# Attention on one core: Q of two quads in one load, in rows of 3 KB

## The chip, the cores and the metric

The kernel runs on one core of a Trainium2 chip. Such a core has five engines with a queue each: TensorE (PE in the profile, its weight loads PEld), VectorE (DVE), ScalarE (ACT), GpSimd (POOL) and SyncE (SP), which only issues transfers here, and 16 DMA engines, which move data between the large memory (HBM) and the on-chip memory (SBUF, 128 partitions). The metric is the device time of one execution in microseconds; the median of several runs counts.

## What is computed

Softmax attention over 16 x 32 = 512 heads, each with 192 queries, 1024 keys and a width of 128, in bf16:

```python
B, H, Sq, Sk, D = 16, 32, 192, 1024, 128

def reference(q, k, v):
    scale = q.shape[-1] ** -0.5
    scores = jnp.einsum("bhqd,bhkd->bhqk", q, k) * scale
    p = _softmax(scores, axis=-1)
    return jnp.einsum("bhqk,bhkd->bhqd", p, v)
```

## The kernel before

**Units.** Four heads make a quad; there are 128 quads (NQ), numbered x. A quad's scores (four heads, 1024 keys by 192 queries, keys along the partitions) are made in three pieces, b = 0, 1, 2, so the unit of the pipeline is f = 3x + b, and there are 384 units (NF). The softmax takes no maximum: ScalarE exponentiates the scores, and a column of ones beside V makes the row sums. A check of the sums at the end would start a slower general path, `_general_path`; it isn't entered with these inputs.

**Loads.** SP issues all loads of the steady state from one queue, in a fixed order: for each n, V of quad n+3 (`load_v`, L555), K of quad n+5 (`load_k`, L546), Q of quad n+5 (`load_q`, L531). K and V are 1 MB a quad, Q is 192 KB. Each load fills all 128 partitions: K with 8 KB in one run per partition, V with four runs of 2 KB, Q with one run of 1536 bytes, which is six rows of Q. K, V and Q have five buffers each (NKN, NVS). K waits for a free buffer on s_kx, V on s_pv. Outputs are stored from ScalarE's queue, two quads at a time, in runs of 768 bytes.

**Preparing K and Q.** [...] VectorE turns 32 x 32 blocks of 4-byte words: `turn_k` (L747) turns a third of a quad's K from f_kn to f_kx, and GpSimd's `order` (L607) copies that third from f_kx to its place in f_kt. Q takes one step: `turn_q` (L756) turns a whole quad's Q and writes it straight to its place in f_qt, which has two buffers (R = 2). So Q's turn writes with a scattered pattern. GpSimd also spreads V into rows with the column of ones (`spread`, L616).

**Order on VectorE.** Its loop runs over f. In each turn it normalises unit f-5 (`onorm`: L768 the reciprocal, L772 the product, both read f_o), and then prepares K for unit g = f+3 (AHEAD = 3). `turn_q(x)` comes right ahead of `turn_k(3x+2)`, so half a dozen microseconds after the first third of the same quad's K.

**Order on GpSimd.** For each x: `order(3x)`, the two halves of `spread(x-1)`, `order(3x+1)`, `order(3x+2)`. It runs strictly in that order: if V of quad x-1 isn't there, the next thirds of K wait too.

**Order on TensorE.** For each f: `qk(f)`, the scores (L654), then `pv(f-4)`, the product with V (L683). `qk` first takes what it needs from counters, each by a wait that also subtracts: s_qt (Q turned, for b = 0 only), s_kt (K in place), s_e1 (the score bank is free). `take` is at L637. `pv` takes s_on, which VectorE's normalisation raises: f_o has one buffer, so `pv(f-4)` can't begin before `onorm(f-5)` has read it.

**ScalarE** exponentiates each unit's scores in two instructions (L838, one head, and L841, three heads).

Of the kernel before, what the change touches and what calls it, by code (L numbers as in the profile page):

```python
# [407 lines left out]
U32 = mybir.dt.uint32  # L408
# [12 lines left out]
def _attention_kernel(nc, q, k, v, out):  # L421
# [4 lines left out]
    NQ = NH // 4  # L426
    T = SK // 128
    scale = float(D) ** -0.5
    R = PE_LOOP
    assert NH % 8 == 0 and NQ >= 12  # L430
    NF = 3 * NQ
    LAG = 4
# [3 lines left out]

    AHEAD = 3
    NKN, NVS, NKT, NVP = 5, 5, 2, 2
    GQ = 2
    NSO = 3  # L440
    VB = 136
# [9 lines left out]
    with ExitStack() as outer:  # L451
# [7 lines left out]
        s_out = sem("f_out")  # L459
        s_blank = sem("f_blank")  # L460
        s_kn = [sem("f_kn%d" % i) for i in range(NKN)]
        s_qn = [sem("f_qn%d" % i) for i in range(NKN)]
        s_v = [sem("f_v%d" % i) for i in range(NVS)]
        s_st = [sem("f_st%d" % i) for i in range(NSO)]
        s_kx = sem("f_kx")
        s_qt = sem("f_qt")
        s_kt = sem("f_kt")
        s_vp = sem("f_vp")
        s_qk = sem("f_qk")
# [10 lines left out]
        with ExitStack() as es:  # L480
# [9 lines left out]
            kx = sb("f_kx", [128, 2, 2048], U32)  # L490

            kt = sb("f_kt", [128, NKT, 2 * T, 128, 2], BF16)
            qn = sb("f_qn", [128, NKN, 384], U32)

            qt = sb("f_qt", [128, R, 2, SQ, 2], BF16)
            vs = sb("f_vs", [128, NVS, 4, T * D], BF16)
# [32 lines left out]

            def load_q(e, x):  # L530
                e.dma_start(  # L531
                    qn[:, x % NKN, :],
                    qf[4 * x:4 * x + 4].rearrange("a (j u) d -> (a j) (u d)", u=6).bitcast(U32),
                ).then_inc(s_qn[x % NKN], 16)

            hints = {}

# [3 lines left out]
            @block.sync  # L541
            def _(e):
                def load_k(x, lo=0, hi=32):
                    if x >= NKN:
                        e.wait_ge(s_kx, 3 * (x - NKN) + 3)
                    e.dma_start(  # L546
                        kn[:, x % NKN, 64 * lo:64 * hi],
                        kf[4 * x:4 * x + 4].rearrange("a (j r) d -> (a j) r d", r=32)[:, lo:hi, :]
                        .rearrange("p r d -> p (r d)").bitcast(U32),
                    ).then_inc(s_kn[x % NKN], 16)  # L550

                def load_v(x, lo=0, hi=4):
                    if x >= NVS:
                        e.wait_ge(s_pv, 3 * (x - NVS) + 2 + BLANK)
                    e.dma_start(  # L555
                        vs[:, x % NVS, lo:hi, :],
                        vf[4 * x + lo:4 * x + hi].rearrange("a (m t) d -> m a (t d)", t=T),
                    ).then_inc(s_v[x % NVS], 16)


                load_k(0)
                e.wait_ge(s_blank, 1)
                load_k(1)
                load_q(e, 1)
                load_v(0, 0, 2)
                e.wait_ge(s_qk, PRE + 1)
                load_v(0, 2, 4)
                load_k(2, 0, 16)
                e.wait_ge(s_pv, BLANK - 2)
                load_k(2, 16, 32)  # L570
                load_q(e, 2)
                for n in range(3, NKN):
                    load_v(n - 2)
                    load_k(n)
                    load_q(e, n)
                for n in range(NQ):
                    if n == NQ // 2:
                        hint(e)
                    if n + NKN - 2 < NQ:
                        load_v(n + NKN - 2)  # L580
                    if n + NKN < NQ:
                        load_k(n + NKN)
                        load_q(e, n + NKN)
                for i in range(len(store_at), len(stores)):
                    store(e, i)
            def stored(e):
# [3 lines left out]
            @block.gpsimd  # L590
            def _(gp):
                gp.memset(ones[:], 1.0).then_inc(s_one, 1)  # L592

                def set_v(part):
                    return gp.memset(part.bitcast(U32), 0x3F803F80)  # L595

                set_v(vp[:, 0, 0:2 * T].rearrange("p a d -> p (a d)")).then_inc(s_set, 1)
                set_v(vp[:, 0, 2 * T:].rearrange("p a d -> p (a d)")).then_inc(s_blank, 1)
                set_v(vp[:, 1].rearrange("p a d -> p (a d)"))

                def order(g):
                    x, b = divmod(g, 3)
                    lo, hi = PIECES[b]
                    gp.wait_ge(s_kx, g + 1)
                    if x >= NKT - 1 and b == 0:
                        gp.wait_ge(s_qk, 3 * (x - NKT) + 3 + PRE)
                    gp.tensor_copy(  # L607
                        kt[:, x % NKT].bitcast(U32).rearrange("p U (j s u) c -> p U j s (u c)", s=2, u=2)[:, lo:hi],
                        kx[:, x % 2].rearrange("p (U s j u) -> p U j s u", s=2, j=32, u=2)[:, lo:hi],
                    ).then_inc(s_kt, 1)  # L610

                def spread(x, i):
                    if i == 0:
                        gp.wait_ge(s_v[x % NVS], 16 * (x // NVS + (2 if x % NVS == 0 else 1)))
                        gp.wait_ge(s_pv, 3 * (x - NVP) + 3 + BLANK)
                    gp.tensor_copy(  # L616
                        vp[:, x % NVP, 2 * T * i: 2 * T * i + 2 * T, 0:D].bitcast(U32),
                        vs[:, x % NVS, 2 * i: 2 * i + 2, :].rearrange("p a (t d) -> p (a t) d", d=D).bitcast(U32),
                    ).then_inc(s_vp, 1)

                for x in range(NQ + 1):
                    if x == NQ // 2:
                        hint(gp)
                    if x < NQ:
                        order(3 * x)
                    if x >= 1:
                        for i in range(2):
                            spread(x - 1, i)
                    if x < NQ:
                        order(3 * x + 1)  # L630
                        order(3 * x + 2)

            @block.tensor
            def _(pe):
# [3 lines left out]

                def qk(f):
                    x, b = divmod(f, 3)  # L640
                    if b == 0:
                        take(s_qt, 1)
                    take(s_kt, 1)
                    take(s_e1, 1)
                    ins = None
                    for group in CUTS[b]:
                        for w in range(4):
                            h, c = divmod(w, 2)
                            for g, (t, n0, n1) in enumerate(group):
                                c0 = t * SQ + n0 - 512 * b  # L650
                                for a in range(4):
                                    S = s3_ps[f % 2][:, a - 1, :] if a else s1_ps[:]
                                    r = slice(32 * a, 32 * a + 32)
                                    ins = pe.matmul(  # L654
                                        S[:, c0: c0 + n1 - n0],
                                        kt[r, x % NKT, 2 * t + h, :, c],
                                        qt[r, x % R, h, n0:n1, c],
                                        start=w == 0 and g == 0, stop=w == 3, skip_group_check=True,
                                        tile_position=(32 * a, 0))
                    ins.then_inc(s_qk, 1)  # L660
# [57 lines left out]
            def _(dve):  # L718
# [5 lines left out]
                    ins = clear(low[:, z, :, 1, :])  # L724
                ins.then_inc(s_set, 1)
                clear(qt[:, 1].rearrange("p h q c -> p (h q c)"))
                dve.sem_inc(s_e1, 1 + PRE)
                clear(kt[:, 1, 10:16].rearrange("p U k c -> p (U k c)")).then_inc(s_kt, 1)
                for z in range(2):
                    ins = clear(low[:, z, :, 2, :])  # L730
                ins.then_inc(s_out, 1)
                dve.wait_ge(s_out, 2)
                dve.wait_ge(s_blank, 1)
                dve.sem_inc(s_on, LAG + 1 + PRE)
                where = {}
                for i, (x0, c) in enumerate(stores):
                    for a in range(c):
# [2 lines left out]
                def turn_k(g):  # L740
# [8 lines left out]
                        kn[:, x % NKN].rearrange("p (s u U i) -> p s u U i", s=2, u=2, i=32)[:, :, :, lo:hi],  # L749
                    ).then_inc(s_kx, 1)  # L750

                def turn_q(x):
                    dve.wait_ge(s_qn[x % NKN], 16 * (x // NKN + 1))
                    if x >= R - 1:
                        dve.wait_ge(s_qk, 3 * (x - R) + 3 + PRE)
                    dve.transpose(  # L756
                        qt[:, x % R].bitcast(U32).rearrange("p b (y j u) c -> p u y b (j c)", y=3, u=2),
                        qn[:, x % NKN].rearrange("p (u y b i) -> p u y b i", u=2, y=3, b=2),
                    ).then_inc(s_qt, 1)

                def onorm(s):
                    x, w = divmod(s, 3)
# [35 lines left out]
                for f in range(NF + LAG + 1):  # L798
                    s = f - LAG - 1
                    if f == NF // 2:  # L800
                        hint(dve)
                    if s >= 0:
                        onorm(s)
                        if 0 <= s - EARLY < 3:
                            check(0, 2 * EARLY, 0, s - EARLY)
                    g = f + AHEAD
                    if 5 <= g < NF:
                        x, b = divmod(g, 3)
                        if b == 2 and x >= 2:
                            turn_q(x)  # L810
                        turn_k(g)
                for part in range(3):
                    check(2 * EARLY, 2 * NF, 1, part)
# [70 lines left out]
```

## Time and profile before

| | |
|---|---|
| median of 3 runs | 819.04 us (818.56 to 820.16) |
| the profiled execution: its time | 816.7 us |
| the profiled execution: its span | 815.0 us |
| granted TensorE clock | 0.996 |
| read from HBM, written | 293.60 MB, 25.17 MB |

The span runs from the first to the last instruction; the time of the same execution is 1.7 us longer, and the median of the unprofiled runs lies 4.04 us above the span.

The groups of instructions that the change touches, or that stand beside them (line, engine, operation, what it writes and reads, count; then busy time, mean of one in ns, and the idle time just before them with what ended it):

```profile
L747 DVE STREAM_TRANSPOSE f_kx<-f_kn 128x768 uint32<-128x768 uint32 x256 | 248.6, 972 | 38.4 <-DMA f_kn<-in_k_dram 36.5 <-PE f_s L654 1.1
L607 POOL COPY f_kt<-f_kx 128x768 uint32<-128x768 uint32 x256 | 220.9, 863 | 92.1 <-DVE f_kx L747 90.3 <-PE f_o L683 0.2
L747 DVE STREAM_TRANSPOSE f_kx<-f_kn 128x512 uint32<-128x512 uint32 x128 | 85.8, 670 | 0.0
L607 POOL COPY f_kt<-f_kx 128x512 uint32<-128x512 uint32 x128 | 82.2, 642 | 20.4 <-DVE f_kx L747 20.0
L756 DVE STREAM_TRANSPOSE f_qt<-f_qn 128x384 uint32<-128x384 uint32 x128 | 72.9, 570 | 0.0
```

The transfers (KB each, median us from issue to landing):

```profile
f_kn<-in_k_dram SPq DMA_DIRECT2D x127, 1024.0 KB, 18.1
f_vs<-in_v_dram SPq DMA_DIRECT2D x127, 1024.0 KB, 16.3
f_qn<-in_q_dram SPq DMA_DIRECT2D x127, 192.0 KB, 14.2
out_dram<-f_ob ACTq DMA_DIRECT2D x62, 384.0 KB, 9.5
```

### The profile page before, as it was taken

Reading aid. Unit: us, or ns where it says so; the run is one execution under the profiler, and the core shown is the slowest. Engines: PE = TensorE matmul, PEld = TensorE weight load, DVE = VectorE, ACT = ScalarE, POOL = GpSimd, SP = SyncE. Lnnn points to the kernel's source line nnn. Section 1 sums busy time; section 2 is a strip of 40 time slices with the busy share of each in tenths; the row PEclk is TensorE's granted clock in tenths of the full one; section 3 lists DMA queues with packets and bytes.
Section 4 is the critical chain, followed back from the end, with each engine's and each line's share of the span. In section 5 each row is a group of like instructions: output and inputs, shape, how many; then the busy total and the mean of one; then the engine's idle time right before and its main releaser. Section 6 shows DMA issues by size and latency. Waiting matters only on the chain. (4 is left out here: it accounts for less than half of the span.)

```text
span 815.0 us, 71454 instructions
## 1 busy us (share of the span) xinstructions
PE 802.2 (98%) x32996; PEld 716.0 (88%) x32996; DVE 602.0 (74%) x1293; ACT 749.9 (92%) x772; POOL 553.8 (68%) x648
## 2 busy tenths in 40 slices
PE   8899999999999999999999999999999999999997
PEld 7788888888888888888888888888888888888886
DVE  4677777777777777777777777777777777777775
ACT  6799999999999999999999999999999999999995
POOL 5677677667667766766676676676766766766674
PEclk9999999999999999999999999999999999999999
DMA  7999999999999999999999999999999999999992
GB/s 270 396 401 406 408 404 405 409 403 406 409 403 406 408 403 407 407 405 407 407 403 408 407 404 408 406 406 405 407 406 401 396 409 393 388 406 399 393 379 73
DMA packets 138455, 319.16 MB, mean 392 GB/s; under 512 B 7217, under 2 KB 56369, under 8 KB 122161
## 3 DMA queue, kind: packets, MB, share of 16 engines
q1 hardware_dynamic: 105536, 294.22, 91.9%
q10 hardware_dynamic: 32880, 24.58, 9.0%
q14 instruction: 33, 0.26, 0.1%
q8 instruction: 6, 0.10, 0.1%
HBM read 293.60 MB, written 25.17 MB: 391 GB/s over the span
## 5 line engine op out<-in xcount | busy, mean ns | idle before, releaser
L841 ACT ACTIVATE f_pt<-f_s 128x1536 bf16<-128x1536 f32 x384 | 554.6, 1444 | 0.1
L654 PE MATMUL f_s<-f_qt,f_kt 32*128 32x192 bf16 (+1 forms) x20528 | 423.2, 226 | 7.4 <-PEq L637 7.4
L683 PE MATMUL f_o<-f_vp,f_pt 128*64 128x129 bf16 x12368 | 426.8, 222 | 0.4 <-issue 0.2
L683 PEld LDWEIGHTS f_o<-f_vp,f_pt 128*64 128x64 bf16 x12368 | 363.7, 110 | 49.4 <-issue 22.5
L654 PEld LDWEIGHTS f_s<-f_qt,f_kt 32*128 32x128 bf16 x20528 | 349.4, 92 | 44.0 <-issue 9.1
L607 POOL COPY f_kt<-f_kx 128x768 uint32<-128x768 uint32 (+1 forms) x384 | 298.0, 789 | 112.6 <-DVE f_kx L747 110.3
L747 DVE STREAM_TRANSPOSE f_kx<-f_kn 128x768 uint32<-128x768 uint32 (+1 forms) x384 | 334.3, 871 | 38.4 <-DMA f_kn<-in_k_dram 36.5
L616 POOL COPY f_vp<-f_vs 128x1024 uint32<-128x1024 uint32 x256 | 260.1, 1046 | 137.8 <-DMA f_vs<-in_v_dram 129.7
L838 ACT ACTIVATE f_pt<-f_s 128x512 bf16<-128x512 f32 x384 | 229.3, 597 | 56.4 <-PE f_s L654 13.8
L768 DVE RECIPROCAL f_rinv<-f_o 128x2 f32<-128x2 f32 x381 | 64.2, 168 | 156.1 <-PE f_o L683 154.8
L772 DVE TENSOR_TENSOR f_ob<-f_o,f_rinv 128x256 bf16<-128x256 f32 x381 | 161.6, 424 | 13.3 <-DVE f_rinv L768 0.3
L756 DVE STREAM_TRANSPOSE f_qt<-f_qn 128x384 uint32<-128x384 uint32 x128 | 72.9, 570 | 0.0
L825 ACT ACTIVATE f_pt<-f_ones 128x1536 f32<-128x1536 bf16 x3 | 4.2, 1472 | 0.0
L595 POOL MEMSET f_vp<- 128x1088 uint32 (+1 forms) x3 | 3.8, 1312 | 0.0
L683 PE MATMUL f_s<-f_vp,f_pt 128*64 128x129 bf16 x96 | 3.2, 220 | 0.2 <-issue 0.2
L683 PEld LDWEIGHTS f_s<-f_vp,f_pt 128*64 128x64 bf16 x96 | 2.9, 110 | 0.5 <-issue 0.4
L825 ACT ACT_TABLE_LOAD x1 | 1.3, 1283 | 1.2 <-PEq L869 1.2
L696 PE MATMUL f_o<-f_ones 128*128 128x512 bf16 x2 | 1.0, 622 | 1.1 <-POOL f_ones L592 1.1
L720 DVE MEMSET f_pt<- 128x256 uint32 x4 | 1.1, 272 | 0.9 <-PEq L869 0.9
L768 DVE RECIPROCAL f_rinv<-f_s 128x2 f32<-128x2 f32 x3 | 0.5, 171 | 1.4 <-PE f_s L683 1.4
L713 PE MATMUL f_o<-f_bad,f_ones 128*1 128x1 bf16 x1 | 0.2, 165 | 1.3 <-DVEq L814 1.3
L713 PEld LDWEIGHTS f_o<-f_bad,f_ones 128*1 128x1 bf16 x1 | 0.1, 80 | 1.4 <-DVEq L814 1.4
(15 smaller groups left out, 6.8 us busy)
## 6 DMA issues: line engine op xcount, KB each, us to landing
f_kn<-in_k_dram SPq DMA_DIRECT2D x127, 1024.0 KB, 18.1
f_vs<-in_v_dram SPq DMA_DIRECT2D x127, 1024.0 KB, 16.3
f_qn<-in_q_dram SPq DMA_DIRECT2D x127, 192.0 KB, 14.2
out_dram<-f_ob ACTq DMA_DIRECT2D x62, 384.0 KB, 9.5
f_vs<-in_v_dram SPq DMA_DIRECT2D x2, 512.0 KB, 6.4
f_kn<-in_k_dram SPq DMA_DIRECT2D x2, 512.0 KB, 4.7
out_dram<-f_ob SPq DMA_DIRECT2D x1, 384.0 KB, 3.8
out_dram<-f_ob SPq DMA_DIRECT2D x2, 192.0 KB, 2.1
```

The source lines that it names most:

```text
L595: return gp.memset(part.bitcast(U32), 0x3F803F80)
L607: gp.tensor_copy(kt[:, x % NKT].bitcast(U32).rearrange("p U (j s u) c -> p U j s (u c)", s=2, u=2)[:, lo:hi], kx[:, x % 2].rearrange("p (U ...
L616: gp.tensor_copy(vp[:, x % NVP, 2 * T * i: 2 * T * i + 2 * T, 0:D].bitcast(U32), vs[:, x % NVS, 2 * i: 2 * i + 2, :].rearrange("p a (t d) ...
L654: ins = pe.matmul(S[:, c0: c0 + n1 - n0], kt[r, x % NKT, 2 * t + h, :, c], qt[r, x % R, h, n0:n1, c], start=w == 0 and g == 0, stop=w == 3 ...
L683: ins = pe.matmul(O[64 * z: 64 * z + 64, u, 0:129], pt[:, x % R, 2 * y + z, t * SQ + 64 * j: t * SQ + 64 * j + 64], vp[:, x % NVP, (2 * y ...
L747: dve.transpose(kx[:, x % 2].rearrange("p (U s j u) -> p s u U j", s=2, j=32, u=2)[:, :, :, lo:hi], kn[:, x % NKN].rearrange("p (s u U i) ...
L756: dve.transpose(qt[:, x % R].bitcast(U32).rearrange("p b (y j u) c -> p u y b (j c)", y=3, u=2), qn[:, x % NKN].rearrange("p (u y b i) -> ...
L768: dve.reciprocal(ri, O[:, :, 128]).then_inc(s_rc, 1)
L772: dve.tensor_tensor(ob[:, so, 6 * a + 2 * w: 6 * a + 2 * w + 2, :], O[:, :, 0:128], ri.unsqueeze(2).to_broadcast([128, 2, D]), ALU.mult,). ...
L825: return act.activation(part.bitcast(F32), ones[:, 0:1].to_broadcast([128, 2 * T * SQ // 2]), ACT_FN.Copy)
L838: act.activation(pt[:, x % R, 0, c], s1_ps[:], ACT_FN.Exp, scale=scale).then_inc(s_e1, 1)
L841: act.activation(pt[:, x % R, 1:4, c], s3_ps[f % 2][:], ACT_FN.Exp, scale=scale).then_inc(s_e3, 1)
```

## The change

Quads 0 and 1 keep their own loads of 192 KB and their own turns. From quad 2 on, Q of two quads is loaded at once:

- `load_q2(x)`, for even x, is issued right after K of quad x. It consists of four transfers, one for each 32 partitions. Partition 32a + 2j + h gets 12 rows (3072 bytes in one run) of head a of quad x + h. There are three buffers (NQN) of this double size in place of five of the single size.
- `turn_q2(x)` on VectorE turns these 768 words a partition from f_qn to a new tile f_qx, which has two buffers, without rearranging anything. It is placed ahead of `turn_k(3x-1)`.
- `copy_q(x)` on GpSimd, for every quad from 2 on, copies the 384 words of that quad from f_qx to their places in f_qt. It is placed ahead of `order(3x)`.
- `qk` on TensorE no longer takes s_qt: GpSimd's `order(3x)`, which raises s_kt, comes after `copy_q(x)` on the same engine. For quads 0 and 1 other counters of the start stand in (s_e1 and s_on), whose sums stay the same.

```diff
+    NQN = 3
...
-            qn = sb("f_qn", [128, NKN, 384], U32)
+            qn = sb("f_qn", [128, NQN, 768], U32)
+            qx = sb("f_qx", [128, 2, 768], U32)
...
+            def load_q2(e, x):
+                y = x // 2
+                for a in range(4):
+                    e.dma_start(
+                        qn[32 * a:32 * a + 32, y % NQN, :],
+                        qf[4 * x:4 * x + 8].rearrange("(h a) (j u) d -> a j h (u d)", h=2, u=12)[a].bitcast(U32),
+                    ).then_inc(s_qn[y % NQN], 16)
...
                     if n + NKN < NQ:
                         load_k(n + NKN)
-                        load_q(e, n + NKN)
+                        if (n + NKN) % 2 == 0:
+                            load_q2(e, n + NKN)
...
+                def copy_q(x):
+                    gp.wait_ge(s_qx, x // 2)
+                    gp.wait_ge(s_qk, 3 * (x - R) + 3 + PRE)
+                    gp.tensor_copy(
+                        qt[:, x % R].bitcast(U32).rearrange("p b (y j v) c -> p b y j (v c)", y=3, v=4),
+                        qx[:, x // 2 % 2].rearrange("p (v y b j h) -> p h b y j v", v=4, y=3, b=2, h=2)[:, x % 2])
...
                     if x < NQ:
+                        if x >= 2:
+                            copy_q(x)
                         order(3 * x)
...
-                    if b == 0:
-                        take(s_qt, 1)
                     take(s_kt, 1)
...
+                def turn_q2(x):
+                    y = x // 2
+                    dve.wait_ge(s_qn[y % NQN], 64 * (y // NQN + (1 if y % NQN else 0)))
+                    if y >= 3:
+                        dve.wait_ge(s_qk, 3 * (x - 3) + 1 + PRE)
+                    dve.transpose(
+                        qx[:, y % 2], qn[:, y % NQN],
+                    ).then_inc(s_qx, 1)
...
-                        if b == 2 and x >= 2:
-                            turn_q(x)
+                        if b == 2 and x % 2 == 1 and x + 1 < NQ:
+                            turn_q2(x + 1)
                         turn_k(g)
```

More of the change, by code (lines that the diff above doesn't have):

```diff
@@ L461, in _attention_kernel @@
         s_kn = [sem("f_kn%d" % i) for i in range(NKN)]
-        s_qn = [sem("f_qn%d" % i) for i in range(NKN)]
+        s_q0 = [sem("f_q0%d" % i) for i in range(2)]
+        s_qn = [sem("f_qn%d" % i) for i in range(NQN)]
         s_v = [sem("f_v%d" % i) for i in range(NVS)]
@@ L465, in _attention_kernel @@
         s_kx = sem("f_kx")
-        s_qt = sem("f_qt")
+        s_qx = sem("f_qx")
         s_kt = sem("f_kt")
@@ L531, in load_q @@
                 e.dma_start(
-                    qn[:, x % NKN, :],
+                    qn[:, 0, 384 * x:384 * x + 384],
                     qf[4 * x:4 * x + 4].rearrange("a (j u) d -> (a j) (u d)", u=6).bitcast(U32),
-                ).then_inc(s_qn[x % NKN], 16)
+                ).then_inc(s_q0[x], 16)
+            def load_q2(e, x):
[5 more added lines that the diff above has]
+                    ).then_inc(s_qn[y % NQN], 16)
             hints = {}
@@ L570, in _ @@
                 load_k(2, 16, 32)
-                load_q(e, 2)
+                load_q2(e, 2)
                 for n in range(3, NKN):
@@ L574, in _ @@
                     load_k(n)
-                    load_q(e, n)
+                    if n % 2 == 0:
+                        load_q2(e, n)
                 for n in range(NQ):
@@ L726, in _ @@
                 clear(qt[:, 1].rearrange("p h q c -> p (h q c)"))
-                dve.sem_inc(s_e1, 1 + PRE)
+                dve.sem_inc(s_e1, PRE)
                 clear(kt[:, 1, 10:16].rearrange("p U k c -> p (U k c)")).then_inc(s_kt, 1)
@@ L733, in _ @@
                 dve.wait_ge(s_blank, 1)
-                dve.sem_inc(s_on, LAG + 1 + PRE)
+                dve.sem_inc(s_on, LAG - 1)
                 where = {}
@@ L752, in turn_q @@
                 def turn_q(x):
-                    dve.wait_ge(s_qn[x % NKN], 16 * (x // NKN + 1))
-                    if x >= R - 1:
-                        dve.wait_ge(s_qk, 3 * (x - R) + 3 + PRE)
+                    dve.wait_ge(s_q0[x], 16)
+                    if x == 1:
+                        dve.wait_ge(s_qk, PRE)
                     dve.transpose(
-                        qt[:, x % R].bitcast(U32).rearrange("p b (y j u) c -> p u y b (j c)", y=3, u=2),
-                        qn[:, x % NKN].rearrange("p (u y b i) -> p u y b i", u=2, y=3, b=2),
-                    ).then_inc(s_qt, 1)
+                        qt[:, x].bitcast(U32).rearrange("p b (y j u) c -> p u y b (j c)", y=3, u=2),
+                        qn[:, 0, 384 * x:384 * x + 384].rearrange("p (u y b i) -> p u y b i", u=2, y=3, b=2),
+                    ).then_inc(*((s_on, 2 + PRE) if x else (s_e1, 1)))
+                def turn_q2(x):
[6 more added lines that the diff above has]
+                    ).then_inc(s_qx, 1)
                 def onorm(s):
```

## The prediction

> **What bounds the kernel now.** I read the busy shares and the slices first, then the waits in windows along the run, then the timeline where TensorE stalls, and the DMA rows last.
>
> ```profile
> span 815.0 us, 71454 instructions
> PE 802.2 (98%) x32996; PEld 716.0 (88%) x32996; DVE 602.0 (74%) x1293; ACT 749.9 (92%) x772; POOL 553.8 (68%) x648
> ...
> DMA  7999999999999999999999999999999999999992
> ...
> DMA packets 138455, 319.16 MB, mean 392 GB/s; under 512 B 7217, under 2 KB 56369, under 8 KB 122161
> ...
> q1 hardware_dynamic: 105536, 294.22, 91.9%
> q10 hardware_dynamic: 32880, 24.58, 9.0%
> ```
>
> TensorE and the DMA engines are both full, and a busy TensorE proves little. So I ask who waits, early (100 to 200 us) and late (700 to 815 us):
>
> ```profile
> POOL f_vp L616 <- DMA f_vs<-in_v_dram: 1.3, 4, 0.5
> ```
>
> ```profile
> POOL f_vp L616 <- DMA f_vs<-in_v_dram: 27.0, 16, 2.9
> DVE f_rinv L768 <- PE f_o L683: 16.8, 38, 1.3
> DVE f_kx L747 <- DMA f_kn<-in_k_dram: 9.0, 16, 1.5
> ...
> ACT f_pt L838 <- PE f_s L654: 2.5, 6, 0.8
> ```
>
> Early, loads are no concern and TensorE sets the pace: in the timeline around 400 us the first ScalarE activation of a quad starts at 401.29 and that of the second quad after it at 413.61, so 12.32 us for two quads. Late, V and K arrive after their user is ready, and ScalarE begins to wait for TensorE: 0.4, 0.7, 1.6 and 2.5 us in the windows from 400, 500, 600 and 700 us. The loads are a little slower than TensorE and the stock in the buffers has run out. The timeline at 743 us shows how that reaches TensorE:
>
> ```profile
> 743.13 2.03 POOL L616 COPY f_vp<-f_vs 128x1024 uint32<-128x1024 uint32 x2 [2.94 <-DMA f_vs<-in_v_dram]
> ...
> 745.10 1.45 POOL L607 COPY f_kt<-f_kx 128x768 uint32<-128x768 uint32 x2
> ...
> 745.70 0.98 DVE L747 STREAM_TRANSPOSE f_kx<-f_kn 128x768 uint32<-128x768 uint32 x1 [1.47 <-DMA f_kn<-in_k_dram]
> 746.27 1.10 PE L654 MATMUL f_s<-f_qt,f_kt 32*128 32x64 bf16 x64 [0.66 <-PEq L637]
> ```
>
> V lands late, GpSimd spreads it, only then puts K in place (L607), and TensorE's next scores wait 0.66 us. So here the DMA stream sets the end: whatever lengthens it comes out at the end nearly one to one; what shortens it gains only until TensorE's own pace takes over.
>
> That SP "waits for VectorE" at L546 (378.7 us in the waits of its queue) I don't believe: at 401.22 us such an issue ends, while VectorE's last piece of that quad ends only at 401.97. The issue is held by a full queue (median 4.15 us for K), which fits the DMA row of nines.
>
> [...]
>
> **The change, part by part**, for two quads (a pair; there are 63, since quads 0 and 1 keep their own loads).
>
> *Packets.* The two queue rows give the price of a packet. Queue q10 (the stores): 9.0% of 16 x 815.0 us over 32880 packets is 35.7 ns for 748 bytes. Queue q1: 91.9% over 105536 is 113.6 ns for 2788 bytes. The line through both is 7.1 ns plus 0.0382 ns a byte. Before, a pair's Q is 256 packets of 1536 bytes, 256 x 65.7 ns / 16 engines = 1.05 us. After, 128 packets of 3072 bytes, 128 x 124.4 / 16 = 0.995 us. Two more transfers a pair bring 32 semaphore packets (7217 small packets over 451 issues is 16 each), 32 x 7.1 / 16 = 0.014 us. Saved: 0.043 us a pair, 2.7 us in all.
>
> *Ports.* The four transfers go to partitions 0-31, 32-63, 64-95, 96-127. [...] Below, this costs nothing[...]; above, Q takes twice its time, 0.995 us more a pair, 63 us in all. [...]
>
> *SP.* Two more issues a pair at 0.57 us (median of f_qn's issues in the view of that tile). SP sits 4.15 us in the typical K issue, so that hides. If the queue weren't full, it would delay V by 1.1 us in every second quad. V behind a double Q lands 192 KB later, 0.47 us at 406 GB/s, and the next quad gets that back.
>
> *VectorE.* Two turns of 570 ns become one of 768 words. The K turn of 768 words takes 972 ns with a scattered pattern; two Q turns are 1140; a line through the K turns of 512 and 768 words (670, 972) has 1.18 ns a word[...]. I take 0.90. In that step VectorE has 0.34 us of idle time (the timeline's wait of L768), and the turn is 0.33 us longer: it just fits.
>
> *The wait for Q moves.* Before, quad n's Q was turned ahead of turn_k(3n+2), where one unit is a third of a quad; now Q of n and n+1 is turned three units earlier, ahead of turn_k(3n-1), one unit before the first piece of K of quad n. But Q is issued after that K. So late in the run VectorE stands there for one unit (2.05 us), plus what it waits for K already (9.0/16 = 0.56 us), plus 384 KB behind K at 406 GB/s (0.97 us): 3.5 us. Behind it on VectorE stand the K piece, which has 3.2 us to spare (copied by 403.11 us, used at 406.31), and the next normalisation (L768, L772), which frees the one f_o buffer and has none. So TensorE stops as well. This is paid once and not 63 times: after it TensorE runs 3.5 us further behind the loads, and the next Q is there in time. Bounds: 0 if Q lands early, 3.5 once.
>
> *GpSimd.* 126 copies of 384 words. From 642 ns (512 words) and 863 (768): 0.53 us[...]. It lies before the quad's first L607, where GpSimd stands idle 0.78 us for VectorE (timeline, 403.89). Free; without that cover it delays K's pieces by its own length.
>
> *TensorE.* A wait fewer per quad: its score blocks start at 402.20, 404.25, 406.31, 408.36, so the one with the wait is no longer than the others, and it is worth nothing. But at 800.46 us TensorE's block came 0.59 us late, and ScalarE's activation 0.78 after a wait, because turn_q stood behind the check at L784. That goes: -0.7.
>
> *Start.* turn_k(5) now stands behind the first double Q: K of quad 2 landed at 19.1 us, Q 0.97 later, then 0.90 + 0.67 + 0.64 for turn, K piece and copy, so 22.3 us against 20.68 for that score block. ScalarE's stall of 3.14 us near 29 us, for V of quad 1, follows anyway and takes the 1.6 us in.
>
> Sum against the span of 815.0: -2.7 (packets) +46.1 (ports) +3.5 (Q's wait) -0.7 = 861.2 us. The median of the runs is 819.04, 4.04 above the span, so **865 us**.
>
> **Rivals.**
> - *Ports don't bind; the earlier wait eats the packets' gain.* 815.0 - 2.7 + 3.5 - 0.7 = 815.1, so 819.1 as a median: no change. For it: the overlap of packets (shares of 91.9 and 9.0% add to more than one) hints at some slack in the engines.[...]
> - *Faster.* Ports don't bind, and Q lands before VectorE asks, since SP's issues run some 14 us ahead. Then the late stalls shrink by the 2.7 us of packets and the 0.7 at the end: 811.6, a median of 815.6. It decides only while collisions cost under some 25 ns a pair (1.6 us in all) and the new wait stays below 2 us. Against it: K itself, one place ahead of Q, is already late in 16 quads at the end.
> - *Ports bind in full*[...]: 63 us, median 882.
> - *GpSimd's copy is much slower* (over 1.5 us): its cover is gone and K comes late on every quad, 0.7 us x 126 = some 88 us. Little speaks for it.
>
> **How the numbers follow.** Collisions, in part or in full: 0.55 (its own range 835 to 885). Wait eats gain: 0.26, of which 0.16 within 0.2%, 0.06 slower, 0.04 faster. Faster: 0.15. GpSimd and the rest: 0.04, slower except 0.01. A measurement here tells 0.2% (1.6 us) from nothing. Faster 0.19, same 0.17, slower 0.64. The range runs from 815.5, which leaves out the better part of the faster case, to 882.
>
> **What would show it.** Collisions: fewer bytes a second in every slice (some 385 instead of 406 GB/s), waits on V and K from 50 us on, packets fewer by about 6000. No collisions: 406 GB/s as before, and VectorE's new turn waiting on in_q_dram. I am wrong if the pace of the loads doesn't fall, or if the new turn never waits.

## The result, and the profile after

| | before | changed |
|---|---|---|
| median | 818.8 us (4 runs) | 936.21 us (4 runs, 929.39 to 946.24) |
| span of the profiled execution | 815.0 us | 927.7 us |
| ratio | | 1.1411, 95% interval 1.131 to 1.1513 |

The change makes the kernel 14% slower. The forecast had the direction, and charged the most for the transfers to 32 partitions, which the experiments below found at fault; the loss is two and a half times what it said. Some executions of a kernel fall into a slower state: ratios and intervals leave them out (here one of the changed kernel's four), medians do not.

The page of the changed kernel: span, busy time of the engines, busy shares of the DMA engines in 40 slices, GB/s in the same slices, all packets, and the two queues (packets, MB, share of 16 engines):

```profile
span 927.7 us, 71577 instructions
...
PE 814.8 (88%) x32996; PEld 725.0 (78%) x32996; DVE 594.0 (64%) x1230; ACT 756.5 (82%) x772; POOL 652.6 (70%) x774
...
DMA  7999999999999999999999999999999999999991
GB/s 280 350 377 349 362 374 343 350 367 331 354 348 335 355 327 345 338 341 359 337 353 356 358 362 370 359 360 378 354 346 372 342 349 365 344 354 358 352 347 63
DMA packets 132408, 319.18 MB, mean 344 GB/s; under 512 B 9232, under 2 KB 42256, under 8 KB 116112
...
q1 hardware_dynamic: 99488, 294.22, 93.0%
q10 hardware_dynamic: 32880, 24.58, 8.0%
```

The same row of GB/s of the kernel before:

```profile
GB/s 270 396 401 406 408 404 405 409 403 406 409 403 406 408 403 407 407 405 407 407 403 408 407 404 408 406 406 405 407 406 401 396 409 393 388 406 399 393 379 73
```

The DMA engines are as busy as before, with the same megabytes and 6047 packets fewer. But they move about 350 GB/s where they moved about 406, from the second slice on. The load queue's packets took 91.9% of 815.0 = 749 us per engine before, and take 93.0% of 927.7 = 863 us now: 114 us more, against a span that is 113 us longer. So the transfers themselves became slow; nothing was added to them. TensorE's share falls from 98 to 88% (815 us of 928); only GpSimd's rises, from 68 to 70%, with its 126 new copies.

Where the kernel waits (engine, line, what it waited for: us in total, times, longest):

```profile
POOL f_kt L623 <- DVE f_kx L771: 242.0, 135, 4.8
...
DVE f_qx L792 <- DMA f_qn<-in_q_dram: 120.7, 62, 7.5
PE f_o L707 <- PEq L663: 102.6, 61, 4.0
ACT f_pt L876 <- PE f_o L707: 94.6, 61, 4.2
...
POOL f_vp L639 <- DMA f_vs<-in_v_dram: 12.7, 28, 1.8
...
DVE f_kx L771 <- DMA f_kn<-in_k_dram: 4.1, 2, 3.0
```

The late loads no longer show at V and K but at Q, once per pair of quads, because Q's turn is now the first in VectorE's order that needs a new load. One such place in the timeline (start, duration, engine, line, operation, idle time before it and what ended that):

```profile
424.92 0.98 DVE L792 STREAM_TRANSPOSE f_qx<-f_qn 128x768 uint32<-128x768 uint32 x1 [2.26 <-DMA f_qn<-in_q_dram]
...
425.82 0.67 DVE L771 STREAM_TRANSPOSE f_kx<-f_kn 128x512 uint32<-128x512 uint32 x1
426.42 0.13 DVE L803 RECIPROCAL f_rinv<-f_o 128x2 f32<-128x2 f32 x1
...
427.15 1.10 PE L707 MATMUL f_o<-f_vp,f_pt 128*64 128x129 bf16 x32 [2.08 <-PEq L663]
427.66 1.45 ACT L876 ACTIVATE f_pt<-f_s 128x1536 bf16<-128x1536 f32 x1 [1.94 <-PE f_o L707]
```

VectorE waits 2.26 us for Q, turns it and a piece of K, and only then normalises (L803), with no idle time before it: it is late. TensorE needs f_o free and stands 2.08 us. Two readings fit this. Either the loads are slow and this is merely where it shows, or the early wait holds TensorE up and the loads follow. The experiments had to tell them apart.

### The profile page after: what moved, and what is told of

It is laid out like the page before. It is cut to its first block, busy times and chain, and to the rows that moved or that the text cites. A ratio compares the mean times of both kernels' runs of the same rounds, so it can differ in the third digit from the quotient of the medians.

```text
span 927.7 us, 71577 instructions
## 1 busy us (share of the span) xinstructions
PE 814.8 (88%) x32996; PEld 725.0 (78%) x32996; DVE 594.0 (64%) x1230; ACT 756.5 (82%) x772; POOL 652.6 (70%) x774
## 5 line engine op out<-in xcount | busy, mean ns | idle before, releaser
L707 PE MATMUL f_o<-f_vp,f_pt 128*64 128x129 bf16 x12368 | 431.6, 223 | 103.6 <-PEq L663 102.6
L707 PEld LDWEIGHTS f_o<-f_vp,f_pt 128*64 128x64 bf16 x12368 | 369.5, 111 | 155.7 <-issue 135.8
L678 PE MATMUL f_s<-f_qt,f_kt 32*128 32x192 bf16 (+1 forms) x20528 | 427.8, 228 | 4.6 <-PEq L663 4.0
L803 DVE RECIPROCAL f_rinv<-f_o 128x2 f32<-128x2 f32 x381 | 62.6, 164 | 190.7 <-PE f_o L707 190.7
L807 DVE TENSOR_TENSOR f_ob<-f_o,f_rinv 128x256 bf16<-128x256 f32 x381 | 161.7, 424 | 13.3 <-DVE f_rinv L803 0.3
L792 DVE STREAM_TRANSPOSE f_qx<-f_qn 128x768 uint32<-128x768 uint32 x63 | 61.6, 978 | 120.7 <-DMA f_qn<-in_q_dram 120.7
L631 POOL COPY f_qt<-f_qx 128x384 uint32<-128x384 uint32 x126 | 111.4, 884 | 0.0
L807 DVE TENSOR_TENSOR f_ob<-f_s,f_rinv 128x256 bf16<-128x256 f32 x3 | 1.3, 424 | 0.1
```

Of the source, the lines that this page charges most:

```text
L631: gp.tensor_copy(qt[:, x % R].bitcast(U32).rearrange("p b (y j v) c -> p b y j (v c)", y=3, v=4), qx[:, x // 2 % 2].rearrange("p (v y b j ...
L678: ins = pe.matmul(S[:, c0: c0 + n1 - n0], kt[r, x % NKT, 2 * t + h, :, c], qt[r, x % R, h, n0:n1, c], start=w == 0 and g == 0, stop=w == 3 ...
L707: ins = pe.matmul(O[64 * z: 64 * z + 64, u, 0:129], pt[:, x % R, 2 * y + z, t * SQ + 64 * j: t * SQ + 64 * j + 64], vp[:, x % NVP, (2 * y ...
L792: dve.transpose(qx[:, y % 2], qn[:, y % NQN],).then_inc(s_qx, 1)
L803: dve.reciprocal(ri, O[:, :, 128]).then_inc(s_rc, 1)
L807: dve.tensor_tensor(ob[:, so, 6 * a + 2 * w: 6 * a + 2 * w + 2, :], O[:, :, 0:128], ri.unsqueeze(2).to_broadcast([128, 2, D]), ALU.mult,). ...
```

## The experiments

What was expected is told by theories. The "ports theory" says that a transfer that fills only 32 of the 128 partitions slows the loads, those of K and V among them; the name is the author's guess at a cause, and no trace here shows a port. The "halves theory" says this of every transfer that stays within partitions 0 to 63 or 64 to 127, and of no other. The "visitors theory" is a second guess: that it matters which of the DMA engines writes a partition, and not the half. The trace doesn't tell the engine.

### The width of Q's transfers, with the early turn and the copy kept

Two transfers of 192 KB over all 128 partitions, in runs of 1536 bytes, in place of four over 32, with GpSimd's copy reading the layout that follows from it:

```diff
-                for a in range(4):
+                for h in range(2):
                     e.dma_start(
-                        qn[32 * a:32 * a + 32, y % NQN, :],
-                        qf[4 * x:4 * x + 8].rearrange("(h a) (j u) d -> a j h (u d)", h=2, u=12)[a].bitcast(U32),
+                        qn[:, y % NQN, 384 * h:384 * h + 384],
+                        qf[4 * x + 4 * h:4 * x + 4 * h + 4].rearrange("a (j u) d -> (a j) (u d)", u=6).bitcast(U32),
...
```

> The changed kernel, but Q of two quads comes in two transfers of 192 KB over all 128 partitions (1536-byte runs, as before) in place of four over 32 partitions; turn, place of the turn and GpSimd's copy stay. Ports theory[...]: all of the loss goes, 817 to 823 us, the shares of q1 back to about 750 us per engine. Wait theory (VectorE's early turn stops TensorE once per pair, and the loads only follow): stays at 925 to 945 us. Count theory (four small transfers cost as such): also about 820.

Measured: 818.52 us, ratio to before 1.0005 (0.9994 to 1.0017). The early turn and the copy are in it, and the loss is gone: the early wait isn't the cause. Its load queue on the page:

```profile
q1 hardware_dynamic: 105536, 294.22, 91.5%
```

That is 750 us per engine at its span of 819.9.

### The narrow transfers alone, in the kernel before

```diff
-                e.dma_start(
-                    qn[:, x % NKN, :],
-                    qf[4 * x:4 * x + 4].rearrange("a (j u) d -> (a j) (u d)", u=6).bitcast(U32),
-                ).then_inc(s_qn[x % NKN], 16)
+                for a in range(4):
+                    e.dma_start(
+                        qn[32 * a:32 * a + 32, x % NKN, :],
+                        qf[4 * x + a].rearrange("(j u) d -> j (u d)", u=6).bitcast(U32),
+                    ).then_inc(s_qn[x % NKN], 16)
```

> The kernel before, but each quad's Q comes in four transfers over 32 partitions (1536-byte runs), nothing else changed: eight such transfers per pair of quads. Ports theory: [...] most of its loss, 915 to 950 us. Wait theory: no loss, 818 to 822 us. Count theory: twice the transfers of the changed kernel, so over 1000 us.

Measured: 912.01 us, ratio 1.1109 (1.1058 to 1.116), just below the 915 to 950 us of the ports theory. The narrow transfers alone make about four fifths of the loss, with the old turn in its old place. Where the last fifth comes from no run tells; the runs here have 1536 bytes and those of the change 3072. Eight narrow transfers per pair cost no more than the change's four, so their number isn't it. Here the waits stand at V and K again:

```profile
POOL f_vp L617 <- DMA f_vs<-in_v_dram: 259.4, 127, 3.5
DVE f_kx L748 <- DMA f_kn<-in_k_dram: 198.9, 128, 4.5
ACT f_pt L839 <- PE f_s L655: 130.2, 215, 1.9
```

### As many small transfers, but wide

Four transfers of 96 KB per pair, each over 128 partitions in runs of 768 bytes:

```diff
+                for i in range(4):
+                    h, w = divmod(i, 2)
+                    e.dma_start(
+                        qn[:, y % NQN, 192 * i:192 * i + 192],
+                        qf[4 * x + 4 * h:4 * x + 4 * h + 4].rearrange("a (j u) d -> (a j) (u d)", u=6)[:, 384 * w:384 * w + 384].bitcast(U32),
...
```

> The changed kernel with four transfers of 96 KB per pair of quads, as many as it has, but each over all 128 partitions (768-byte runs); turn, its place and GpSimd's copy stay. Count theory (four small transfers cost as such, by issue or by semaphore): 900 us or more. Ports theory: no collision, only 8064 x 2 more packets than with 1536-byte runs, 7 ns each on 16 engines, about 7 us more than the run with two full-width transfers (818.5): 820 to 830 us.

Measured: 826.79 us, ratio 1.0125 (1.0108 to 1.0142). Against the run with two wide transfers it has 123680 - 105536 = 18144 packets more in the load queue. At the forecast's 7.1 ns on 16 engines that is 8.1 us. The medians differ by 8.3 us; but they were taken at different times, and the two ratios to the kernel before differ by 0.0120, which is 9.8 us. So the price of a packet holds roughly, and a small transfer as such costs little more.

### Which partitions a narrow transfer reaches

Four kernels leave all of the change as it is and differ only in how the same 3072-byte runs are grouped into transfers:

```diff
 # order of the four groups
-                for a in range(4):
+                for a in (0, 2, 1, 3):
...
 # two halves
-                        qn[32 * a:32 * a + 32, y % NQN, :],
+                        qn[64 * a:64 * a + 64, y % NQN, :],
...
 # every fourth partition
+                        qn[s:128:4, y % NQN, :],
...
 # every second partition of a half
+                        qn[64 * g + t:64 * g + 64:2, y % NQN, :],
```

Order 0, 2, 1, 3:

> The changed kernel with the four transfers issued in the order 0, 2, 1, 3 of their partition groups[...]. Ports theory, if the loss comes from all engines crowding one half while the other rests: a part comes back, 870 to 910 us. Ports theory[...]: no difference, 925 to 950 us. Wait theory and count theory: no difference either.

Two transfers of 64 partitions:

> The changed kernel with two transfers of 64 partitions in place of four of 32; same runs of 3072 bytes, same places. [...] Visitors theory[...]: about half of the loss, 860 to 890 us. Halves theory[...]: the loss stays, 910 to 945 us.

Every fourth partition:

> The changed kernel with four transfers of 32 partitions each, but every fourth partition[...]; same runs of 3072 bytes, same places. Halves theory: no loss, 813 to 822 us. Visitors theory: [...] most of the loss stays, 890 to 940 us.

Every second partition of one half:

> The changed kernel with four transfers of 32 partitions, every second partition of one half (0 to 62, 1 to 63, 64 to 126, 65 to 127); same runs of 3072 bytes, same places. Halves theory: [...] the loss stays, 905 to 945 us. Neighbours theory (what hurts is that neighbouring partitions are written one after another, and the step of four cured it): no loss, 813 to 822 us.

| a transfer's partitions | transfers per pair | reach, by partition number | median, us | ratio to before |
|---|---|---|---|---|
| 32 neighbours (the change) | 4 | one half | 936.21 | 1.1411 (1.131 to 1.1513) |
| 32 neighbours, halves in turn | 4 | one half | 912.21 | 1.1149 (1.1086 to 1.1211) |
| 64 neighbours | 2 | one half | 941.89 | 1.1531 (1.146 to 1.1602) |
| every second of a half, 32 | 4 | one half | 933.63 | 1.12 to 1.14 (three runs, 918.52 to 934.2; no interval) |
| every fourth of all, 32 | 4 | both halves | 814.54 | 0.9975 (0.9961 to 0.9989) |

This is the clearest of the results. Four transfers of 32 partitions cost nothing at all when they are spread over all 128. They cost 11 to 15% when each stays within 64 neighbours, whether it takes all of these, 32 in a row or every second one. A transfer of 64 neighbours fares no better than one of 32: 941.89 us against 936.21. The visitors theory fell by its numbers: it had 860 to 890 us for two transfers of 64, and 890 to 940 for every fourth partition, where 941.89 and 814.54 were measured. Letting the halves take turns seems to bring back a fifth: its 912.21 us, from two runs only, lie between the two ranges that were expected, 870 to 910 and 925 to 950, and decide for neither.

The page of the every-fourth run:

```profile
span 814.0 us, 71577 instructions
...
DMA packets 132408, 319.18 MB, mean 392 GB/s; under 512 B 9232, under 2 KB 42256, under 8 KB 116112
...
q1 hardware_dynamic: 99488, 294.22, 91.3%
```

Instructions, packets and bytes are those of the changed kernel to the last digit; only which of the 3072-byte runs share a transfer differs. 91.3% of 814.0 is 743 us per engine against 863, and the spans differ by 113.7 us.

Whose packets became slow is told by the packets' own records in the trace (mean ns of one packet in the load queue):

| | Q, 3072 B, x8064 | V, 2048 B, x65536 | K, 8192 B, x16256 |
|---|---|---|---|
| every fourth partition | 122.0 | 85.8 | 314.5 |
| the change | 172.0 | 100.5 | 347.1 |
| the difference, over 16 engines | 25 us | 60 us | 33 us |

Q's own packets carry 25 of some 118 us. The rest lies on K and V, which were not touched. The same records tell when: sort the packets of K and V by how many of Q's were in flight as each began.

| mean ns of one packet | no Q packet in flight | six or more |
|---|---|---|
| K in the change | 318.4 | 482.3 |
| K with every fourth partition | 315.0 | 310.0 |
| V in the change | 89.7 | 135.6 |
| V with every fourth partition | 86.2 | 84.3 |

So K and V are held up while narrow Q packets are on their way, and hardly otherwise. The Q packets of a transfer don't run all at once: some were in flight for about 428 us of the changed kernel's execution, six or more for only 78. In the every-fourth run that was 298 and 64 us, so there too Q runs beside K and V, and slows neither. Why the grouping makes this difference the records don't say.

### The wait, moved later

Q is turned ahead of turn_k(3x+1) of its own quad, one loop step after that quad's first piece of K, and TensorE takes s_qt again:

```diff
-                        if b == 2 and x % 2 == 1 and x + 1 < NQ:
-                            turn_q2(x + 1)
+                        if b == 1 and x % 2 == 0:
+                            turn_q2(x)
...
+                        if x >= 2 and x % 2 == 1:
+                            copy_q(x)
                         order(3 * x)
+                        if x >= 2 and x % 2 == 0:
+                            copy_q(x)
```

With the four narrow transfers:

> The changed kernel with its four narrow transfers, but Q is turned three units of the loop less two later, after the first third of K of the same quad, and GpSimd copies it after that third; TensorE takes the Q counter again. If VectorE's wait for Q is only where the late loads show: no gain, 920 to 945 us, and the waiting moves to K and V. If the early place adds to the loss by itself: 900 to 915 us, as in the kernel before with narrow transfers (912).

Measured: 927.37 us, ratio 1.1322 (1.1258 to 1.1385), which overlaps the change's interval. The waiting moved:

```profile
DVE f_kx L776 <- DMA f_kn<-in_k_dram: 182.3, 114, 5.5
POOL f_vp L640 <- DMA f_vs<-in_v_dram: 155.3, 121, 2.6
```

So the 120.7 us at Q were the place where slow loads surfaced, with no cost of their own that this comparison can see.

### One wide transfer in runs of 3072 bytes

Head and row group of HBM can be named together, since they lie at one step. Then all 128 partitions are reached by one transfer, with the change's own runs and places:

```diff
-                for a in range(4):
-                    e.dma_start(
-                        qn[32 * a:32 * a + 32, y % NQN, :],
-                        qf[4 * x:4 * x + 8].rearrange("(h a) (j u) d -> a j h (u d)", h=2, u=12)[a].bitcast(U32),
+                e.dma_start(
+                    qn[:, y % NQN, :],
+                    qf[4 * x:4 * x + 8].rearrange("(h a) (j u) d -> (a j) h (u d)", h=2, u=12).bitcast(U32),
...
```

> The changed kernel with the same 3072-byte runs and the same places, but as one transfer over all 128 partitions (head and row group taken together as the outermost size, 64). Ports theory: no loss; the packets' gain of 2.7 us and the earlier wait of 3.5 us stand against each other, 815 to 821 us. Wait theory: stays at 925 to 945 us.[...]

> The one transfer of 3072-byte runs over all 128 partitions once more, beside the next run: 812 to 816 us, 0.4 to 0.6% below the kernel before.

Measured: 814.44 us, ratio 0.9949 (0.9929 to 0.9968), and again 814.18 us, 0.995 (0.9927 to 0.9972). It is the fastest kernel of the study, half a per cent below the kernel before; the every-fourth run is next to it. Its waits from 100 to 800 us:

```profile
DVE f_rinv L802 <- PE f_o L706: 167.4, 284, 0.8
POOL f_kt L622 <- DVE f_kx L770: 121.1, 168, 1.4
PEld f_o L706 <- issue: 18.7, 116, 0.2
DVE f_qx L791 <- DMA f_qn<-in_q_dram: 0.4, 2, 0.3
ACT f_pt L872 <- PE f_s L677: 0.4, 2, 0.2
```

In the long middle loads make nobody wait, but for 0.4 us at Q; what remains are engines that wait for TensorE and for each other. The late stalls of the kernel before are gone. TensorE paid for the early wait at the start, in one stop:

```profile
32.23 0.98 DVE L791 STREAM_TRANSPOSE f_qx<-f_qn 128x768 uint32<-128x768 uint32 x1 [2.73 <-DMA f_qn<-in_q_dram]
...
34.46 0.73 PE L706 MATMUL f_o<-f_vp,f_pt 128*64 128x129 bf16 x19 [2.55 <-PEq L662]
```

### The same with the late turn

> The one transfer of 3072-byte runs over all 128 partitions, and Q turned after the first third of K of the same quad, with TensorE's own wait for Q back. If the early wait costs TensorE once, at the start (2.55 us at 34.46 us in the profile of the one-load run), that comes back: 2 to 4 us below the one-load run, 809 to 812 us. If the start is set by the loads alone, the stop only moves: equal within 1 us.

Measured: 816.24 us, ratio 0.998 (0.9968 to 0.9992): 2 us slower than the early turn, a miss. Its timeline says why:

```profile
406.48 0.97 DVE L796 STREAM_TRANSPOSE f_qx<-f_qn 128x768 uint32<-128x768 uint32 x1
406.85 1.10 PE L711 MATMUL f_o<-f_vp,f_pt 128*64 128x129 bf16 x32
...
407.37 0.94 DVE L775 STREAM_TRANSPOSE f_kx<-f_kn 128x768 uint32<-128x768 uint32 x1
...
408.23 0.13 DVE L807 RECIPROCAL f_rinv<-f_o 128x2 f32<-128x2 f32 x1
...
408.97 1.10 PE L711 MATMUL f_o<-f_vp,f_pt 128*64 128x129 bf16 x32
```

The later place has the large piece of K behind it, 0.94 us in place of 0.67 or 0.70. The normalisation (L807) starts without any idle time, and TensorE's two blocks lie 2.12 us apart where 2.05 is its pace. Some 0.07 us in each of 63 pairs is 4 to 5 us, more than the stop of 2.55 us that the late turn spares.

## Why the forecast was right in kind and wrong in size

- **What bounds the kernel** held: a longer load stream came out at the end one to one (114 us of packet time, 113 us of span).
- **Ports: the term that failed.** The forecast charged 46.1 us, 0.73 us a pair, to Q's packets only. That was the author's assumption, as was the doubling of Q's time in the upper bound: the trace of the kernel before, whose loads all fill 128 partitions, doesn't show what a narrower one costs. By the every-fourth run the narrow grouping costs 113.7 / 63 = 1.80 us a pair. Q's own packets grew by 25 us, 0.40 a pair, less than charged; the other 93 us or so are K and V. The forecast named waits on V and K as a sign of collisions, and then priced only Q; the packets of K and V that began with six or more of Q's in flight took half as long again as those that began with none (482.3 against 318.4 ns, 135.6 against 89.7). Its upper bound of 0.995 us, Q at twice its time, was no bound for the same reason, so the range ended at 882.
- **Packets** held: 7.1 ns each. The one-load run has 9072 fewer than the run with two wide transfers, 4.0 us by that price; the medians, from one batch, differ by 4.1. A packet of 3072 bytes took 122.0 ns in the every-fourth run, where the forecast had 124.4.
- **The wait for Q** held in kind: without the narrow transfers' loss TensorE stopped for it once, for 2.55 us. But it came at the start, not late in the run, and 3.5 was said (its terms, 2.05, 0.56 and 0.97, make 3.58). The turn of before stood two units, 4.1 us, behind the first third of its quad's K, not half a dozen microseconds. Its place in the sum was wrong too. It was set against the packets' gain, for no change; in the profile of the one-load run ScalarE waited for TensorE 2.7 us more than before in the first 100 us (11.4 against 8.7), but 4.7 us less after that (0.4 against 5.1). The fewer packets have a large part in this: in the run with two wide transfers, with the same early turn and as many packets as before, ScalarE still waited 4.3 us after the first 100. Whether the later start of TensorE, which gives the loads a lead, adds to it isn't shown.
- **The rivals**, for a kernel without that loss: "no change" (0.26) was wrong, and the number of "faster" (0.15) was right, 3.4 us forecast and 3.6 measured in the one-load run. That is luck in part, since its reason, that Q lands before VectorE asks, did not hold at the start: VectorE waited for Q for 9.4 us in the first 100.
- **VectorE's turn**: 0.90 forecast, 978 ns measured; it fits beside the small piece of K, and the late-turn run shows that it doesn't beside the large one. **GpSimd's copy**: 0.53 us by its size from the copies of K, 884 ns measured (592 in the run with two wide transfers, where it reads the other layout); hidden, as the one-load run shows. **SP's issues**: hidden, as the every-fourth run shows, which has as many as the change.
- **What would show it** was half wrong. The fall in GB/s came (some 355 against the 385 expected), but the waits stood at Q, which the forecast had kept as the sign of no collisions.

What is still open: the packets' records have queue, time and size, but neither the DMA engine nor the partition. What K's and V's packets wait for while Q's are in flight is therefore not shown. Nor is it shown that the partitions alone decide. With its partitions, each grouping also changes which rows of HBM a transfer reads: those that lose read one or two heads of a quad at a time, and those that lose nothing read all four. No run separates the two. Shown is that the grouping of the runs into transfers decides, and that every grouping within one half of the partitions lost.

## What to carry to other kernels

When the DMA engines are as full as here (91.9% in the load queue and 9.0% in the stores' before), judge a transfer by which partitions it reaches (or which rows of HBM it reads, which no run here separates) and not only by its bytes and runs: spread over all 128, four transfers of Q took 814.54 us, within one half of them 912 to 936. Keep each one spread, as here, in one transfer (814.44 us) if HBM's layout allows it. Price a collision on everything that is in flight beside the transfer, not only on the transfer that causes it: Q's own packets carried 25 of some 118 us. And where loads are late, the wait shows at whoever needs the next load first (120.7 us at Q in the change, 182.3 at K and 155.3 at V with the later turn); move that wait before you call it the cause.

## What was not expected of the hardware

Moving 8% of the loaded bytes (24.8 of 294 MB) through one half of the partitions at a time lowered the whole stream from about 406 to about 350 GB/s. Packets of 8192 bytes that nobody had touched went from 314.5 to 347.1 ns in the mean, and to 482.3 where they began with six or more of Q's in flight. As many partitions per transfer, 32, at a step of four cost nothing (814.54 us, 0.9975 of before).
